# A linear-attention block gated by a mixer: the tables of order and places replaced by tables searched over replays with late adding transfers

## The chip, the cores and the metric

The kernel runs on one core of a Trainium2 chip. The metric is the device time of one execution in microseconds (us). The engines are PE (TensorE, matrix products), ACT (ScalarE), DVE (VectorE), POOL (GpSimd) and SP (SyncE, which here only issues transfers). Each engine takes its own instructions strictly in the order in which the kernel issues them; engines wait for one another by semaphores. A transfer (DMA) is issued by an engine and lands some microseconds later. An *adding transfer* is one that POOL issues and that adds what it brings to what the destination tile holds already; the program calls it a gather.

## The reference

The input x has 2048 rows of 512. It is normalised, sent through linear attention with 32 heads and, beside that, through a mixer with a token shift; the one gates the other.

```python
xn = _layernorm(x)
# s: linear attention, 32 heads of width 16
pq, pk = phi(q), phi(k)            # phi(t) = t+1 if t>0 else exp(t), plus 1e-6
kv = einsum("bhsd,bhse->bhde", pk, v);  z = einsum("bhsd->bhd", pk)
s = (einsum(pq, kv) / (einsum(pq, z) + 1e-6)) @ wo
# g: mixer
h  = gelu(_layernorm(xn) @ w1)     # four quarters of its columns, shifted by +1, -1, +2, -2 rows
x1 = xn + shifted(h) @ w2
g  = silu(x1 + gelu(_layernorm(x1) @ w3) @ w4)     # w3: 512 x 1376
return x + s * g
```

## The kernel before, in words

**How the work is cut.** The 2048 rows are four blocks of 512, each four tiles of 128. Products are kept at full accuracy by splitting each factor into a rounded high part and a remainder (names that end in h and l): three matmuls for each product, all through the helper `mm` (L133). Where it can, the kernel computes a two-by-two block product with seven products in place of eight (`pair_kq` for keys and queries, `seven` for the mixer and the up projection, `down_late` for the down projection).

**The operations.** The program doesn't issue instructions as it goes. It fills a `Plan`: each helper records an operation with its engine, and the plan works out which tiles it reads and writes. The helpers, with the lines that the profile shows: `mm` L133 (PE), `act` L155 (ACT), `tt` L178, `ts` L183 and `stt` L188 (DVE, or POOL where said so), `load` L194, `store` L199 and L201, `fetch` L206 (all three on SP) and `gather` L212 (POOL, the adding transfer). In all there are 5664 operations: 3315 on PE, 860 on DVE, 845 on ACT, 153 on POOL and 491 on SP.

**The order and the places.** At the end stand two tables written out by hand. `ORDER_OF_ALL` (from L1600) lists the numbers of all 5664 operations; `PLACES` lists, for each of the 1782 tiles, which buffer of its pool it gets (90 buffers of tag p, 6 of h, 12 of sm, 2 of w, 2 of ab, and 4 + 4 PSUM banks acc and mm; -1 where there is nothing to choose). `emit` goes through the table of order and issues each operation on its engine; so each engine's own order is the table with the other engines left out. A tile that takes over a buffer has to wait for the readers of the tile that had it before.

**Two stretches that the prediction speaks of.**

Around 80 to 105 us the kernel handles the key and query products of block 3 (rows 1536 on) and gets ready for the mixer on block 0. The tile xt3_c holds a quarter of block 3 transposed (`load_u`): SP loads it, POOL adds the row of means (`nrow`) by a gather (operations 744, 748, 752 and 756 for c = 0 to 3), and ACT and DVE split it into u3_ch and u3_cl (operation 745 is ACT's u3_0h). `forms_x` makes the sums xs3_n from them (operation 788 is ACT's xs3_0h). `pair_kq(12)` multiplies them: operation 899 is PE's first product with u3_0h, 906 the one with xs3_0h. `load_halo` fetches two small pieces of `nrow` into hm (operations 1134 and 1135 on SP), POOL adds them to hal (1136), and ACT rounds hal to halh (1137). `scale_x` computes the mean terms nm1 on POOL (762 and 763) that ACT needs for the normalisation of x12 (764). Operation 610 is an adding transfer of one key tile into zacc, 1122 the one into xt0_1, a tile of block 0 that `load_u(0, 1)` loads a second time.

Around 440 to 460 us the down projection of block 3 (`down_late`) is on. Its results xo14 and xo15 get the stored x1 added by gathers (operations 4938 and 4962), then `gate` takes the silu on ACT (th14, operation 4939) and multiplies by the attention on DVE (4940). Beside it `down_forms(0)` makes the factors for the next block: operation 5007 is ACT's rounding d_s40h, 5008 DVE's remainder d_s40l.

At about 199 us PE waits for ACT's o7 (operation 1798), with operation 1872 the first product behind the wait; both are in `mix2`.

Of the kernel before, what the change touches and what calls it, by code (L numbers as in the profile page):

```python
# [245 lines left out]
def linear_attn_gated_by_mixer(  # L246
# [1341 lines left out]
    for b in LINE:  # L1588
# [11 lines left out]
        0, 16, 1, 5, 20, 11, 3, 15, 12, 4, 13, 17, 2, 23, 14, 32, 6, 18, 19, 45, 44, 35, 21, 97, 22, 26, 46, 98,  # L1600
        174, 47, 53, 123, 24, 29, 48, 33, 108, 175, 25, 99, 49, 100, 34, 38, 102, 96, 124, 103, 51, 105, 41, 50,
        106, 109, 36, 107, 56, 125, 110, 27, 246, 52, 178, 126, 176, 37, 28, 101, 54, 62, 104, 301, 111, 112, 59,
        179, 30, 113, 55, 158, 10, 31, 117, 127, 118, 186, 177, 119, 142, 65, 39, 240, 159, 128, 180, 143, 114, 66,
        505, 42, 160, 40, 203, 57, 181, 161, 237, 144, 145, 43, 129, 115, 67, 474, 247, 116, 162, 130, 146, 68, 187,
        147, 260, 58, 120, 121, 248, 69, 131, 163, 182, 122, 243, 204, 70, 164, 132, 8, 165, 74, 135, 205, 264, 71,
        206, 75, 183, 63, 220, 221, 9, 188, 166, 60, 207, 7, 222, 76, 167, 223, 64, 224, 256, 225, 72, 77, 194, 61,
        148, 241, 149, 78, 189, 136, 268, 133, 137, 83, 226, 480, 238, 197, 227, 190, 84, 198, 73, 138, 150, 184,
        200, 242, 199, 79, 477, 195, 284, 85, 168, 244, 483, 228, 201, 139, 239, 86, 285, 245, 191, 169, 286, 192,
        250, 88, 287, 208, 151, 91, 89, 209, 249, 210, 196, 92, 152, 193, 134, 202, 140, 211, 80, 212, 288, 251,
        232, 81, 281, 309, 282, 170, 278, 279, 153, 185, 252, 229, 272, 303, 253, 475, 273, 255, 275, 87, 304, 280,  # L1610
        493, 171, 337, 213, 95, 302, 476, 338, 254, 276, 277, 154, 349, 214, 230, 90, 289, 481, 257, 290, 274, 305,
        155, 291, 261, 283, 172, 292, 215, 328, 269, 339, 296, 156, 325, 293, 294, 482, 306, 265, 326, 327, 310,
        321, 231, 141, 340, 319, 216, 341, 733, 342, 402, 334, 93, 233, 329, 295, 478, 404, 331, 322, 332, 313, 335,
        330, 94, 336, 217, 343, 307, 344, 317, 345, 346, 297, 403, 258, 333, 347, 484, 348, 314, 357, 354, 234, 259,
        409, 360, 355, 262, 487, 350, 405, 410, 315, 358, 361, 366, 263, 362, 406, 311, 411, 407, 412, 390, 367,
        546, 497, 413, 266, 392, 363, 82, 414, 386, 501, 547, 312, 548, 394, 408, 356, 388, 415, 416, 395, 368, 417,
        396, 364, 423, 479, 369, 397, 418, 365, 419, 485, 267, 157, 430, 431, 420, 316, 270, 421, 432, 370, 389,
        433, 359, 393, 424, 486, 422, 271, 434, 373, 425, 426, 400, 387, 427, 488, 435, 371, 428, 401, 442, 429,
        443, 318, 444, 298, 445, 391, 173, 446, 447, 308, 489, 549, 490, 550, 235, 398, 551, 492, 553, 320, 436,
        554, 727, 555, 556, 236, 399, 323, 509, 557, 1133, 558, 437, 448, 449, 450, 510, 559, 451, 438, 452, 453,  # L1620
        378, 454, 372, 579, 580, 439, 581, 455, 381, 511, 582, 552, 583, 324, 611, 494, 456, 617, 459, 440, 460,
        379, 560, 498, 461, 351, 462, 463, 382, 512, 464, 352, 561, 562, 465, 502, 299, 584, 563, 567, 469, 568,
        513, 569, 374, 620, 470, 570, 506, 571, 457, 572, 526, 377, 614, 441, 564, 300, 380, 565, 471, 724, 618,
        619, 522, 751, 621, 472, 622, 458, 612, 573, 531, 629, 385, 615, 218, 495, 616, 730, 586, 585, 491, 566,
        587, 613, 623, 496, 574, 626, 635, 466, 630, 575, 631, 588, 514, 636, 535, 589, 590, 576, 627, 591, 375,
        624, 628, 592, 499, 625, 637, 473, 542, 632, 500, 633, 593, 638, 639, 530, 640, 503, 534, 634, 532, 596,
        641, 706, 536, 709, 538, 467, 597, 598, 603, 599, 533, 600, 468, 539, 540, 649, 747, 650, 601, 518, 541,
        703, 656, 657, 725, 577, 521, 700, 642, 743, 602, 658, 537, 659, 525, 594, 660, 726, 661, 353, 643, 543,
        644, 595, 662, 645, 604, 646, 578, 507, 701, 647, 504, 675, 383, 605, 676, 677, 376, 606, 710, 678, 544,
        704, 755, 607, 679, 648, 680, 796, 545, 651, 728, 707, 508, 652, 731, 705, 668, 681, 2027, 669, 734, 702,  # L1630
        797, 384, 711, 732, 653, 885, 737, 670, 654, 529, 735, 798, 517, 671, 672, 729, 799, 685, 686, 655, 736,
        687, 688, 519, 673, 803, 738, 674, 689, 663, 690, 708, 608, 664, 800, 804, 805, 609, 806, 692, 739, 715,
        759, 740, 801, 693, 691, 718, 742, 719, 760, 712, 219, 802, 807, 808, 694, 515, 713, 1121, 714, 817, 809,
        741, 721, 761, 722, 665, 810, 762, 1134, 811, 682, 812, 666, 988, 813, 861, 748, 695, 716, 717, 818, 696,
        756, 829, 723, 830, 697, 831, 763, 720, 523, 814, 832, 744, 1135, 864, 815, 819, 752, 816, 820, 821, 870,
        776, 683, 822, 610, 833, 865, 823, 516, 867, 684, 868, 834, 824, 886, 698, 871, 862, 772, 872, 869, 520,
        836, 764, 775, 837, 524, 866, 1117, 838, 879, 887, 767, 757, 839, 825, 876, 1136, 877, 882, 785, 863, 835,
        840, 841, 749, 873, 842, 880, 1137, 881, 1138, 883, 784, 874, 853, 1122, 846, 758, 878, 745, 847, 848, 780,
        884, 667, 875, 782, 788, 849, 850, 783, 826, 899, 789, 900, 1151, 906, 843, 786, 907, 1118, 908, 746, 768,
        851, 909, 750, 910, 790, 771, 911, 901, 787, 1171, 902, 912, 827, 973, 1129, 903, 1149, 904, 794, 779, 888,  # L1640
        964, 791, 974, 905, 965, 932, 795, 753, 970, 967, 852, 699, 854, 933, 920, 913, 1147, 889, 934, 527, 921,
        781, 922, 844, 923, 792, 924, 925, 890, 1157, 935, 754, 936, 895, 971, 968, 528, 926, 1002, 897, 1003, 793,
        845, 937, 1004, 855, 939, 896, 891, 914, 915, 940, 1123, 898, 975, 966, 856, 828, 972, 941, 769, 1069, 942,
        857, 943, 1130, 1068, 1005, 969, 858, 916, 944, 917, 1125, 859, 918, 985, 1006, 945, 979, 919, 1007, 1067,
        980, 938, 976, 956, 977, 949, 989, 1150, 1124, 982, 1162, 1153, 986, 1154, 987, 1119, 957, 1009, 860, 983,
        1008, 950, 892, 951, 958, 777, 952, 984, 1103, 1010, 978, 1023, 765, 953, 1011, 1148, 1139, 766, 954, 927,
        1012, 1013, 1014, 928, 1016, 1024, 778, 1025, 929, 1017, 1126, 1018, 1015, 981, 2132, 930, 1079, 1266, 1085,
        1161, 1141, 770, 1019, 955, 1070, 1035, 1086, 1120, 1036, 959, 893, 1037, 1026, 946, 1027, 960, 2026, 1028,
        931, 773, 1087, 1104, 947, 1088, 961, 1089, 1090, 1268, 1038, 1029, 962, 1020, 1100, 894, 1155, 1039, 1159,
        990, 1160, 1040, 774, 1042, 1075, 1082, 1083, 991, 1043, 1071, 992, 1021, 1044, 993, 1131, 1045, 1041, 1046,  # L1650
        1142, 1047, 1169, 994, 1101, 1048, 1080, 1158, 1081, 1073, 1172, 1269, 1076, 1084, 1022, 1052, 1053, 1074,
        1054, 1059, 1094, 1055, 1072, 1030, 1056, 1214, 995, 1165, 1091, 1140, 1077, 1095, 1057, 1031, 963, 1200,
        1049, 1215, 1060, 1097, 1127, 1098, 1201, 1078, 1058, 1173, 1061, 1174, 1256, 1202, 1132, 998, 1175, 1267,
        1096, 1167, 1105, 1176, 1152, 1261, 1032, 1092, 1128, 1102, 1000, 1143, 1203, 1163, 999, 1186, 1146, 1062,
        1216, 1187, 1106, 1166, 1177, 1001, 1145, 1170, 1107, 1217, 2036, 1204, 1108, 1218, 1144, 1033, 1188, 1109,
        1099, 1205, 2038, 2037, 1189, 1111, 1274, 1190, 1191, 1050, 1113, 1219, 1034, 1178, 1110, 1206, 2142, 1115,
        1207, 1294, 1063, 1278, 997, 1220, 1093, 2029, 1192, 1064, 1208, 2039, 1221, 1275, 1193, 1179, 1180, 1065,
        1181, 1209, 1210, 2028, 1051, 1211, 2030, 1182, 1183, 1114, 1408, 1222, 1223, 948, 1184, 1224, 1225, 1288,
# [352 lines left out]
```

## Time and profile before

| | us |
|---|---|
| median of three executions | 501.97 (501.96, 501.97, 503.74) |
| the profiled execution | 504.37 |
| its span (first to last instruction) | 502.7 |

| engine | busy, us | share of the span |
|---|---|---|
| PE | 492.8 | 98% |
| DVE | 436.8 | 87% |
| ACT | 381.0 | 76% |
| POOL | 109.7 | 22% |

Rows of the profile read like this. In a timeline: the start in us, the duration in us, the engine, the line, the instruction, the tiles as out<-in (buffer numbers left out: xo stands for xo0 to xo15), the shape, and in square brackets how long the engine sat idle before and what it waited for. In a list of waits: who waited, for whom, the total in us, how often, and the longest. "DMA to landing" is the time from a transfer's issue to its landing. In a windows row: the stretch, its length, the busy time of PE, of weight loads, DVE, ACT and POOL (with the count of instructions), the granted PE clock, the DMA share and GB/s. Matmuls overlap, so what a PE row costs is the distance from one start to the next, and not its duration.

### The profile page before, as it was taken

To read this page: it belongs to the slowest core of one execution; us is meant where nothing else is said; L and a number is where in the kernel's file an instruction comes from. 1 tells how busy PE (TensorE), PEld (TensorE's weight loads), DVE (VectorE), ACT (ScalarE), POOL (GpSimd) and SP (SyncE) were. 2 spreads that over 40 slices of the span, in tenths; PEclk is the share of its full clock that TensorE was granted. 3 is DMA by queue.
4 is the path that set the end of the run, shared out by engine and by line. 5 is a ranking of instruction groups with operands and counts; after the bars stand their busy time and mean duration, and the time that the engine had idled before them with its cause. 6 is when DMAs were issued, how large, how long until landed. Compare 5 with 4: busy or idle time off the path is not lost.

```text
span 502.7 us, 10103 instructions
## 1 busy us (share of the span) xinstructions
PE 492.8 (98%) x3340; PEld 447.9 (89%) x3340; DVE 436.8 (87%) x860; ACT 381.0 (76%) x904; POOL 109.7 (22%) x157
## 2 busy tenths in 40 slices
PE   8999999999999999999999999999999999999996
PEld 5777777778787988988999999999999999999996
DVE  6999985688999988999999899999989979876754
ACT  5999999587976898998899777566679557556421
POOL 1674514322110222211011000000000044334330
PEclk9999999999999999999999999999999999999999
DMA  7978897999988989869798788757779989999998
GB/s 227 356 177 182 177 281 257 229 238 254 303 224 259 209 277 217 220 172 267 213 250 260 276 254 255 223 176 213 242 240 303 322 175 259 272 204 265 274 236 237
DMA packets 90925, 121.59 MB, mean 242 GB/s; under 512 B 10745, under 2 KB 42393, under 8 KB 90873
## 3 DMA queue, kind: packets, MB, share of 16 engines
q1 hardware_dynamic: 78488, 98.93, 60.9%
q0 software_dynamic: 12384, 22.03, 26.7%
q8 instruction: 26, 0.43, 0.3%
q14 instruction: 27, 0.21, 0.1%
HBM read 74.63 MB, written 42.09 MB: 232 GB/s over the span
## 4 chain that ended last, share of the span: by engine, by line
PE 51%; DVE 10%; DMA 5%; issue 3%; ACT 3%; POOL 1%; SPq 0%; DVEq 0%; ACTq 0%; POOLq 0%
PE pb L133 10%; PE pbd L133 9%; PE pe L133 5%; PE ped L133 5%; PE pbs L133 4%; PE h L133 3%; PE pad L133 3%; PE pa L133 3%; PE pbm L133 2%; DMA xo<-x1d 2%; PE pes L133 2%; PE a L133 2%; DMA y_0t<-y_0d 2%; PE pem L133 1%; PE pas L133 1%
## 5 line engine op out<-in xcount | busy, mean ns | idle before, releaser
L212 POOL DMA_DIRECT2D xo<-x1d x12 | 11.7, 989 | 151.4 <-DVE xo L178 133.4
L155 ACT ACTIVATE th<-xo 128x512 f32<-128x512 f32 (+1 forms) x16 | 9.8, 615 | 29.1 <-DMA xo<-x1d 13.5
L212 POOL DMA_DIRECT2D o<-xnd x16 | 14.1, 896 | 73.6 <-DVE o L178 42.1
L212 POOL DMA_DIRECT2D zacc<-ke x12 | 11.7, 975 | 47.5 <-DMA zacc<-ke 7.9
L212 POOL DMA_DIRECT2D th<-in_x x14 | 12.8, 940 | 32.1 <-DVE th L188 12.8
L212 POOL DMA_DIRECT2D xt<-nrow x16 | 15.2, 1169 | 7.3 <-DMA nrow<-ar 3.4
L155 ACT ACTIVATE ht<-ht 128x512 f32<-128x512 f32 x16 | 9.7, 624 | 4.8 <-DVE ht L178 4.7
L155 ACT ACTIVATE y<-o,nm,rs 128x512 f32<-128x512 f32 x16 | 12.7, 810 | 0.0
L183 POOL TENSOR_SCALAR w<-mv 128x4 f32<-128x4 f32 (+2 forms) x10 | 2.9, 292 | 42.5 <-ACT sq L155 42.2
L188 DVE SCALAR_TENSOR_TENSOR th<-th,so 128x512 f32<-128x512 f32 x8 | 5.5, 689 | 7.6 <-ACT th L155 7.6
L178 DVE TENSOR_TENSOR ht<-h,abc 128x512 f32<-128x512 f32 x16 | 10.9, 685 | 1.2 <-PE h L133 1.0
L155 ACT ACTIVATE sq<-o,mv 128x512 f32<-128x512 f32 x16 | 11.6, 723 | 0.2
L188 DVE SCALAR_TENSOR_TENSOR qz<-pq,zb 128x512 f32<-128x512 f32 x16 | 10.9, 682 | 0.6 <-ACT zb L155 0.4
L155 ACT ACTIVATE pa<-pb 128x256 f32<-128x256 f32 x20 | 7.4, 371 | 5.0 <-PE pb L133 4.7
L188 DVE SCALAR_TENSOR_TENSOR pq<-pq,rd 128x512 f32<-128x512 f32 x16 | 10.9, 682 | 0.2
L1283 DVE TENSOR_REDUCE den<-qz 128x32 f32<-128x512 f32 x16 | 10.8, 676 | 0.2
L155 ACT ACTIVATE p<-pe 128x256 f32<-128x256 f32 x20 | 7.5, 377 | 4.5 <-PE pe L133 4.5
L452 POOL TENSOR_TENSOR rs<-w,nhalf 128x4 f32<-128x4 f32 (+2 forms) x10 | 10.3, 1031 | 0.8
L155 ACT ACTIVATE sq<-o 128x512 f32<-128x512 f32 x16 | 10.0, 626 | 0.1
L155 ACT ACTIVATE x<-x,nm,rs 128x512 f32<-128x512 f32 x12 | 9.4, 803 | 0.0
L155 ACT ACTIVATE u<-pb 128x256 f32<-128x256 f32 x20 | 7.6, 380 | 2.3 <-PE pb L133 2.3
L188 DVE SCALAR_TENSOR_TENSOR qr<-qe,qi 128x512 f32<-128x512 f32 x10 | 6.8, 688 | 2.8 <-PE pbx L133 2.7
(2020 smaller groups left out, 2477.8 us busy)
## 6 DMA issues: line engine op xcount, KB each, us to landing
w_s<-in_w SPq DMA_DIRECT2D x23, 256.0 KB, 4.6
x<-in_x SPq DMA_DIRECT2D x16, 256.0 KB, 5.3
xt<-in_xt SPq DMA_DIRECT2D x16, 256.0 KB, 4.5
xnd<-x SPq DMA_DIRECT2D x16, 256.0 KB, 3.6
xt<-nrow POOLq DMA_DIRECT2D x16, 256.0 KB, 7.5
pqd<-qr SPq DMA_DIRECT2D x16, 256.0 KB, 4.4
pq<-pqd SPq DMA_DIRECT2D x16, 256.0 KB, 3.2
o<-xnd POOLq DMA_DIRECT2D x16, 256.0 KB, 5.3
```

What stands on the lines that cost most here:

```text
L133: lambda: nc.tensor.matmul(out.get(), lhs.get(), rhs.get(), start=start, stop=stop, skip_group_check=more))
L155: nc.scalar.activation(out.get(), src.get(), func, scale=get(scale), **kw)
L178: self.vec(eng, out, [a, b], lambda: self.e(eng).tensor_tensor(out.get(), a.get(), b.get(), op=op), True)
L183: lambda: self.e(eng).tensor_scalar(out.get(), a.get(), get(s1), get(s2), **kw), False,
L188: lambda: self.nc.vector.scalar_tensor_tensor(out.get(), a.get(), get(s), b.get(), op0=op0, op1=op1),
L212: lambda: self.nc.gpsimd.dma_start(out.get(), get(src), accum_op=ALU.add), mb=mb)
L452: lambda: g.tensor_tensor(out.get(), src.get(), nh.get(), op=ALU.pow))
L1283: pl.add("DVE", .6, .68, [t], [den], lambda: nc.vector.tensor_reduce(den.get(), t.get().rearrange("p (h d) -> p h d", d=DH), axis=AX.X, op ...
```

## The change

Both tables are replaced, and nothing else: the functions that record the operations are the same to the letter. The few words that came with the change: the same operations, with tables of order and places searched on over replays in which some adding transfers land several microseconds late.

Taken engine by engine, 2783 of PE's 3315 operations stand at another position (by 3.6 positions on average, 33 at most), 591 of DVE's 860 (1.5 and 17), 607 of ACT's 845 (1.9 and 30), 357 of SP's 491 (2.2 and 17) and 42 of POOL's 153 (0.5 and 6). Of the 1782 places 1469 differ. The core of the diff, with the lines that hold the operations named above (the last pair is the first change in `PLACES`):

```diff
@@ -1597,376 +1597,376 @@
...
-        741, 721, 761, 722, 665, 810, 762, 1134, 811, 682, 812, 666, 988, 813, 861, 748, 695, 716, 717, 818, 696,
-        756, 829, 723, 830, 697, 831, 763, 720, 523, 814, 832, 744, 1135, 864, 815, 819, 752, 816, 820, 821, 870,
-        840, 841, 749, 873, 842, 880, 1137, 881, 1138, 883, 784, 874, 853, 1122, 846, 758, 878, 745, 847, 848, 780,
-        884, 667, 875, 782, 788, 849, 850, 783, 826, 899, 789, 900, 1151, 906, 843, 786, 907, 1118, 908, 746, 768,
...
+        696, 810, 811, 515, 1134, 817, 752, 720, 741, 665, 812, 813, 744, 519, 722, 666, 829, 717, 697, 756, 723,
+        864, 682, 520, 861, 870, 748, 818, 830, 683, 819, 610, 814, 516, 820, 1135, 821, 822, 1117, 1122, 867, 823,
+        868, 831, 684, 832, 762, 815, 836, 763, 816, 865, 837, 838, 523, 862, 833, 824, 834, 524, 863, 871, 764,
+        775, 853, 877, 878, 886, 780, 846, 745, 988, 847, 667, 784, 848, 1129, 875, 785, 757, 880, 881, 788, 758,
+        899, 900, 749, 884, 789, 906, 826, 907, 1171, 782, 849, 779, 786, 908, 1136, 850, 787, 790, 851, 1118, 964,
+        746, 909, 768, 910, 750, 911, 970, 912, 901, 783, 902, 827, 903, 794, 904, 973, 791, 967, 1137, 905, 965,
...
-        1798, 1831, 1710, 1669, 1832, 1803, 1870, 1848, 1749, 1833, 1871, 1872, 1850, 2008, 1873, 1874, 1835, 1886,
...
+        1831, 1737, 1798, 1868, 1869, 1870, 1669, 1832, 1803, 2008, 1848, 1833, 1871, 1872, 1710, 1850, 1873, 1874,
...
-        5062, 4938, 5012, 5084, 4998, 5085, 5086, 5353, 5113, 5063, 5064, 5058, 5065, 5329, 5087, 5001, 4988, 5099,
-        5149, 4963, 5122, 5123, 5161, 5005, 5131, 5162, 5132, 4964, 5163, 5007, 5164, 5165, 5133, 5134, 5011, 5166,
-        4965, 5167, 5135, 4939, 5136, 5168, 5093, 5124, 5137, 5138, 5150, 4940, 5125, 5151, 5380, 5169, 5170, 5126,
-        5111, 5008, 5033, 5139, 4941, 5171, 5172, 5127, 5152, 5387, 5173, 5174, 5175, 5368, 5153, 5140, 5176, 5141,
...
+        5062, 5053, 4938, 4998, 5099, 5079, 4984, 5080, 5129, 5081, 5031, 5082, 5083, 4879, 5054, 5084, 5085, 5100,
+        4939, 5166, 5167, 5355, 5149, 5168, 5007, 5137, 5150, 5151, 5347, 5124, 5380, 5169, 4996, 5170, 5171, 5172,
+        4880, 5093, 5138, 5139, 5140, 5141, 5142, 5125, 5173, 5126, 5008, 5174, 5175, 5152, 5153, 5143, 4940, 5127,
...
-        -1, 79, 76, -1, 1, 3, 2, 14, 0, 35, 50, 53, 58, 60, 55, 62, 76, 81, 71, 74, 84, 88, 59, 65, 77, 83, 19, 20,
...
+        -1, 79, 21, -1, 1, 3, 2, 14, 0, 35, 50, 53, 58, 60, 55, 62, 76, 81, 71, 74, 84, 88, 59, 65, 77, 83, 19, 20,
...
```

711 rows, old and new, of tables (ORDER_OF_ALL, PLACES) are left out of this document.

## The prediction

> **What bounds the kernel now.** I read the page's first part, then the list of TensorE's waits, then the timelines of every engine around the longest waits.
>
> ```profile
> span 502.7 us, 10103 instructions
> PE 492.8 (98%) x3340; PEld 447.9 (89%) x3340; DVE 436.8 (87%) x860; ACT 381.0 (76%) x904; POOL 109.7 (22%) x157
> ```
> ```profile
> PE pbx L133 <- ACT u_0h L155: 1.1, 1, 1.1
> PE warm L133 <- POOL ones L368: 1.0, 1, 1.0
> PE k L133 <- ACT u_1h L155: 0.8, 1, 0.8
> ```
> ```profile
> 498.08 0.28 PE L133 MATMUL pbd<-w_l1h,dl1l 96*128 96x256 f32 x1
> ```
>
> PE is busy 492.8 of 502.7 us, so 9.9 us is idle in all. The waits list splits it: 1.0 (for the constant) and 0.8 (the first u_1h) lie at the very start, and after the last matmul (498.08 + 0.28 = 498.36) the tail takes 502.7 - 498.36 = 4.3. What is left between start and tail is 9.9 - 1.0 - 0.8 - 4.3 = 3.8 us. The tables of order hold the same 3315 PE operations in both kernels, the head (first seven PE operations) and the last fifty PE operations stand as they stood, so start and tail are taken as unchanged and only the 3.8 us are at stake. Each wait costs a little more than its idle time, because the matmuls before it drain; the first of the two places below lists 1.10 and loses 1.26, so 0.16 more. With four such waits of weight (three at the places below and the one that stays) the whole that an order could win is about 3.8 + 4 x 0.16 = 4.4 us. Against the median of 501.97 that is a floor of 497.6.
>
> **Place one, 99 us.** Matmuls of width 512 start 0.23 apart where nothing waits (98.86 to 99.09).
>
> ```profile
> 98.86 0.39 PE L133 MATMUL pbx<-kq_t41h,u_3h 128*128 128x512 f32 x1
> 99.09 0.40 PE L133 MATMUL pbx<-kq_t41l,u_3h 128*128 128x512 f32 x1
> 100.58 0.50 PE L133 MATMUL pbx<-wk_0h,u_0h 128*128 128x512 f32 x1 [1.10 <-ACT u_0h L155]
> ```
> ```profile
> 99.23 0.26 ACT L155 ACTIVATE halh<-hal 128x64 fp32r<-128x64 f32 x1 [2.59 <-POOL hal L178]
> 99.40 0.61 ACT L155 ACTIVATE qe<-qk 128x512 f32<-128x512 f32 x1
> 99.92 0.61 ACT L155 ACTIVATE u_0h<-xt 128x512 fp32r<-128x512 f32 x1
> ```
> ```profile
> 84.73 0.20 POOL L178 TENSOR_TENSOR nm<-mv,ns 128x4 f32<-128x4 f32 x1
> 85.72 1.85 POOL L212 DMA_DIRECT2D xt<-nrow  x2 [0.79 <-PE pex L133]
> 87.65 0.22 POOL L183 TENSOR_SCALAR nm<-nm 128x4 f32<-128x4 f32 x1
> 87.93 1.80 POOL L212 DMA_DIRECT2D xt<-nrow  x2
> 98.72 0.49 POOL L178 TENSOR_TENSOR hal<-hal,hm 128x64 f32<-128x64 f32 x1 [8.09 <-issue]
> 100.03 0.88 POOL L212 DMA_DIRECT2D xt<-nrow  x1
> ```
> ```profile
> DMA to landing us min/median/max: 5.7/8.4/11.1
> ```
> ```profile
> DMA to landing us min/median/max: 4.2/7.2/8.5
> ```
>
> The start of the matmul of u_0h comes 100.58 - 99.09 = 1.49 after the one before it: 1.49 - 0.23 = 1.26 us lost. It waits for ACT's rounding u_0h. ACT works in order, and its rounding of the halo, halh, stood ahead of u_0h: halh sat 2.59 idle for POOL's sum hal, which sat 8.09 for the two small loads of hm (first of the two landing rows: 5.7 and 11.1 us). The second landing row is that of the eight transfers into xt between 84 and 104 us, loads and gathers.
>
> **Place two, 457 us.** Matmuls of width 256 start 0.12 apart.
>
> ```profile
> 445.17 1.22 POOL L212 DMA_DIRECT2D xo<-x1d  x1
> 446.24 1.93 POOL L212 DMA_DIRECT2D xo<-x1d  x1
> ```
> ```profile
> DMA to landing us min/median/max: 6.1/7.7/9.3
> ```
> ```profile
> xo<-x1d POOLq DMA_DIRECT2D x12, 256.0 KB, 6.3
> ```
> ```profile
> 451.86 0.62 ACT L155 ACTIVATE d_s40h<-d0f_s40f 128x512 fp32r<-128x512 f32 x1
> 455.61 0.63 ACT L155 ACTIVATE th<-xo 128x512 f32<-128x512 f32 x1 [3.13 <-DMA xo<-x1d]
> 456.14 0.36 ACT L155 ACTIVATE u2d<-pbd 128x256 f32<-128x256 f32 x1
> ```
> ```profile
> 456.27 0.69 DVE L188 SCALAR_TENSOR_TENSOR th<-th,so 128x512 f32<-128x512 f32 x1 [2.66 <-ACT th L155]
> 456.88 0.68 DVE L178 TENSOR_TENSOR d_s40l<-d0f_s40f,d_s40h 128x512 fp32r<-128x512 f32 x1
> ```
> ```profile
> 456.19 0.28 PE L133 MATMUL pbd<-wu_40l,d_s1xh 128*128 128x256 f32 x1
> 456.56 0.38 PE L133 MATMUL pbd<-wu_01h,d_s30h 128*128 128x256 f32 x1
> 457.13 0.28 PE L133 MATMUL ped<-wf_b220l,d_s40h 128*128 128x256 f32 x1
> 457.62 0.39 PE L133 MATMUL ped<-wf_b220h,d_s40l 128*128 128x256 f32 x1 [0.21 <-DVE d_s40l L178]
> ```
>
> The adding transfer into xo14 (POOL, 446.24) landed 9.3 us later, at 455.5; the other one in this stretch took 6.1, and the median of all twelve is 6.3. ACT's th14 waited 3.13 for it, DVE's th14 behind that 2.66. Behind ACT's th14 stood u2d, and PE lost 456.56 - 456.19 - 0.12 = 0.25; behind DVE's th14 stood d_s40l, and PE lost 457.62 - 457.13 - 0.12 = 0.37. Together 0.62.
>
> **The change part by part.** Nothing is added or removed: the same 5664 operations, with the same instruction each, so the busy time of PE (492.8) has no term. What changes is which operation stands ahead of which on each engine, and which buffer a tile has (1469 of 1782 places), that is, which earlier reader a write has to outwait.
>
> *Halo behind u_0h.* halh moves nine ACT positions later, behind u_0h and xs_0h. Those two no longer stand behind POOL's 98.72. What is late next is u_0h's own input, its adding transfer. POOL now issues block 3's four gathers in the order 2, 0, 3, 1, all ahead of the two small nm steps; the last of the four was issued by 87.93 + 1.80 = 89.7 before, and the new order takes no longer to that point (the steps of 84.73 and 87.65, 0.20 and 0.22, go behind it). With 7.2 us, the median of xt's row, all four are there at 96.9, with 8.5 at 98.2; ACT needs about 0.6 for each. xt3_1, which was among the earlier ones, is now last; its products come after those of u_0h and xs_0h on PE, 0.23 each after 99.3, and with the median landing u3_1h is done at 97.5. On 8.5 it would be done at 98.8, still ahead. So the 1.26 goes in full. halh itself is needed only by the halo's copies for a later stage, and the rows show no waiter of it beside POOL's second half. Bounds: 0 (u_0h is as late for another reason) to 1.26; I take 1.26, as no row shows u_0h's input late at its old place: ACT's wait was for hal, not for xt.
>
> *xo14's gather one or more places earlier.* On POOL, xo15 and xo14 now go out so that xo14's takes at latest the place of the row at 445.17, 1.07 earlier. With the same 9.3 it lands at 454.4; ACT's th14 is done at 455.1, and d_s40h, which now stands behind th14 (it was at 451.86, ahead), at 455.7. DVE's d_s40l now stands ahead of th14's multiply and is done at 455.7 + 0.7 = 456.4, 0.7 before 457.13, the start of the last matmul ahead of the one that needs d_s40l. So both losses go, 0.62, if the transfer behaves as in this execution. It need not: an execution where xo14's landing takes the 6.3 of the median has it at 452.5, before anything waits for long, and loses nothing here. One late landing in a profiled execution 2.40 us over the median is thin evidence for the median; I count the half, 0.31. The cover is thinner than before in one respect: d_s40h now has th14 ahead of it, so from a landing of about 10 us at the new place PE waits for d_s40h as well.
>
> *The rest.* I expect the many other moves (on average 3.6 positions on PE, 1.5 on DVE) to be neutral, between -2.5 (all that remains of the 4.4 after these two places) and +2.5 (two new waits of the size of place one).
>
> *What stays.* One more stall is left alone by the tables.
>
> ```profile
> 198.84 0.40 PE L133 MATMUL m<-wo_0h,kvrl 128*128 128x512 f32 x1
> 199.97 0.39 PE L133 MATMUL pam<-w_b21h,ha122h 128*128 128x256 f32 x1 [0.73 <-ACT o L155]
> ```
> ```profile
> 200.00:225.00 25.00, 24.69 (x169) 22.33 (x170) 22.58 (x44) 23.76 (x67) 6.08 (x9) 1.00 0.81 208
> 450.00:475.00 25.00, 24.70 (x206) 24.29 (x206) 17.50 (x36) 13.06 (x30) 7.79 (x9) 1.00 1.06 264
> ```
>
> PE loses 199.97 - 198.84 - 0.23 = 0.90 there, and the order of ACT and PE around it is the same in both tables. Behind it DVE is busy 22.58 and ACT 23.76 of 25 us, so this stretch has little room to take up a head start.
>
> **Sum.** -1.26 - 0.31 = -1.57, from the median: 501.97 - 1.57 = 500.4. The profiled execution itself took 504.37 (span 502.7 and 1.67 around it), which is 2.40 above the median; with both places in full it would be 504.37 - 1.88 = 502.5.
>
> **Against the Trainium skill.** The landing rows are 6.1, 6.3 and 9.3 us for 256 KB. The Trainium skill, page "DMA: Bandwidth & Descriptors", section "Anatomy of one DMA — SWDGE (gpsimd) path", fits a transfer that GpSimd issues as about 2.0 us and its bytes over 436e3; for 262,144 bytes that is 2.6 us, an estimate by that page. By it nothing would land late in either order, the change would have nothing to gain, and the time would stay at 501.97. The trace disagrees at every row of this form that is shown here, by more than a factor of two.
>
> **The rivals.**
>
> *No gain (0.18).* In a median execution the landings are shorter than in the profiled one: 5.7 instead of 11.1 for the second load of hm, 5.4 less, would have hal start at 98.7 - 5.4 = 93.3, halh with it, and u_0h not held. Then place one isn't lost in the median either, and taking it away gives nothing. Or the head start at 99 us is used up where DVE and ACT are nearly full. For it: the profiled execution is 2.40 over the median. Against: ACT and POOL wait 2.59 and 8.09, and 2.6 us would have to vanish. Time: 501.97 less at most place two's half, 501.7 to 502.0. The fit of the Trainium skill's page leads to the same time.
>
> *More (0.20).* The order was rearranged almost everywhere, and the other small waits go too. All but the stall at 199 us: 4.4 - 0.9 = 3.5, so 501.97 - 3.5 = 498.5.
>
> *A gather that blocks POOL (0.12), slower.* POOL now has the gather into xt0_1 (row 100.03) ahead of the nm steps (rows 84.73 and 87.65). POOL works in order, and that gather must wait for the plain load of the same tile:
>
> ```profile
> 85.21 0.41 SPq L194 DMA_DIRECT2D xt<-in_xt  x1
> ```
> ```profile
> L155 ACT ACTIVATE x<-x,nm,rs 128x512 f32<-128x512 f32 x12 | 9.4, 803 | 0.0
> ```
>
> Behind nm stand on ACT three normalisations (0.80 each), two exponentials (0.61 each) and then u_0h (0.61). If the load lands L after 85.21, u_0h is done at 85.21 + L + 0.88 + 0.42 + 2.4 + 1.2 + 0.61 = 90.7 + L. PE needs it at about 99.3, so this decides from L = 8.6, which is just over the longest of the xt row, 8.5. Hm's 11.1 gives 11.1 - 8.6 = 2.5 lost in place of 1.26: 501.97 - 0.31 - 1.26 + 2.5 = 502.9. Three us more (as xo14's 9.3 stands over 6.3), 14.1, gives 505.9, which is this rival's price. Against it: the median of xt's landings is 7.2. The row of 100.03 shows only that the load took under 14.8.
>
> **How the numbers follow.** Forecast 0.50 at 500.4, more 0.20 at 498.5, no gain 0.18 at 501.8, the blocked POOL 0.12 at 505.9 (502.9 at its near end). The low end is the floor, 497.6. The high end is 503.7, which the blocked POOL reaches at L = 11.9; above it I leave 0.10, and some below the floor and in the rest. A difference from no change can be told from about 0.5% on, 2.5 us: below 499.46 lie most of "more" and about a fifth of the forecast's spread, 0.18 + 0.10 = 0.28; above 504.48 nearly all of the blocked POOL, 0.11; between them 0.61.
>
> **What would show it.** Right: the matmul of u_0h follows its forerunner by about 0.23 (not 1.49), with halh later on ACT; th14's landing leaves no wait in front of d_s40l; and the 0.90 at the pam matmul stands as before. Wrong: idle time before x12 on ACT or before nm on POOL near 90 us for an xt0_1 load; a new wait of PE over 1 us for any ACT rounding; PE idle between start and tail still near 3.8.

## The result, and the profile after

The new kernel takes 498.3 us in the median of five executions (497.6 to 499.99), the kernel before, run beside it, 503.41 (501.96 to 503.74): a ratio of 0.991, with a 95% interval of 0.9884 to 0.9937. Measured a second time on the chip of the last experiments (`e12_new_again` below) it was 497.95 against 502.63, a ratio of 0.9917 (0.9899 to 0.9935). So the change takes 0.8 to 0.9% off, 4.2 to 4.5 us at the level of 502. (The ratio isn't that of the two medians: in the first measurement these stand 5.1 apart, in the second 4.7.) The profiled execution of the new kernel took 497.6, the lowest of its five; that of the kernel before, 504.37, was longer than any of the five beside it. So the two profiles lie further apart, 6.8 us, than the kernels do.

First the head of the page and TensorE's list of waits (who, for whom, us in total, times, longest):

```profile
span 495.9 us, 10093 instructions
PE 488.3 (98%) x3340; PEld 447.6 (90%) x3340; DVE 436.8 (88%) x860; ACT 380.7 (77%) x904; POOL 108.8 (22%) x157
```
```profile
PE k L133 <- ACT u_1h L155: 1.2, 1, 1.2
PE warm L133 <- POOL ones L368: 1.0, 1, 1.0
PE m L133 <- DVE o L178: 0.4, 1, 0.4
PE pam L133 <- ACT o L155: 0.4, 1, 0.4
```

Only four entries are left: the two of the start, and two of the stall near 196 us that both kernels have. The span is 6.8 us shorter, and 4.5 us of that is *busy* time of PE (492.8 to 488.3), although the matmuls are the same. So "busy" holds waiting too (a row of width 512 lasts 0.39 where the next starts after 0.23), and the idle column doesn't show the whole loss.

Place one in the new kernel, in the timelines of PE and ACT: u_0h's matmul follows its forerunner by 0.23 (it was 1.49), and ACT starts on u_0h 1.5 us before that matmul, at 96.52, and has it 0.9 ahead.

```profile
97.77 0.39 PE L133 MATMUL g<-k10h,x10l 128*128 128x512 f32 x1
98.00 0.39 PE L133 MATMUL pbx<-wk_0h,u_0h 128*128 128x512 f32 x1
```
```profile
96.52 0.62 ACT L155 ACTIVATE u_0h<-xt 128x512 fp32r<-128x512 f32 x1
```

The transfers did not become punctual. The landing row of the tiles xt, 80 to 106 us, says 6.0, 7.7 and 10.0 us (before: 4.2, 7.2 and 8.5):

```profile
DMA to landing us min/median/max: 6.0/7.7/10.0
```

Place two is gone as well. xo15 and xo14 go out at 435.59 and 438.45 (before: 445.17 and 446.24), land 6.0 and 6.7 later, at 441.6 and 445.1, and ACT gets to them 3.5 and 1.3 us after that, with no idle time in front (POOL, the landing row of xo, ACT):

```profile
435.59 0.86 POOL L212 DMA_DIRECT2D xo<-x1d  x1 [3.90 <-ACT xo L155]
438.45 0.86 POOL L212 DMA_DIRECT2D xo<-x1d  x1
```
```profile
DMA to landing us min/median/max: 6.0/6.4/6.7
```
```profile
445.12 0.62 ACT L155 ACTIVATE th<-xo 128x512 f32<-128x512 f32 x1
446.47 0.62 ACT L155 ACTIVATE th<-xo 128x512 f32<-128x512 f32 x1
```

The same shows in the group of these sixteen ACT operations. Its row (busy and mean, then idle time before it and who ended it), first before, then after: 13.5 us of waiting for the adding transfers into xo, and then none of it among the releasers listed. Other profiles told below agree: 8.7 and 8.0 us in two with the old order there, 0.8 in the second one of the new kernel.

```profile
L155 ACT ACTIVATE th<-xo 128x512 f32<-128x512 f32 (+1 forms) x16 | 9.8, 615 | 29.1 <-DMA xo<-x1d 13.5 <-DVE xo L188 8.2 <-DVE xo L178 6.0
```
```profile
L155 ACT ACTIVATE th<-xo 128x512 f32<-128x512 f32 (+1 forms) x16 | 9.8, 614 | 14.0 <-DVE xo L188 7.8 <-PE pbd L133 3.1 <-DVE xo L178 2.2
```

**Where the time went.** For every matmul I took the distance to the next start and subtracted what that form takes where nothing waits (about 0.233 for width 512 and 0.118 for 256). What is left is PE's loss, waits hidden in "busy" included. The level of a row hangs on these values, as a thousandth of a us on each of 2549 matmuls of width 256 is 2.5 us; the differences between columns hang on them by two or three tenths at most. In stretches of 20 or more us of PE's work (not of the clock, so that the kernels can be laid side by side), in us; a star marks stretches in which the kernel of that column has the old order:

| PE's work, us | before | e1 | e6 | e5 | after | after, again |
|---|---|---|---|---|---|---|
| 0–20 (start) | 2.26* | 2.81* | 2.54* | 2.23 | 2.35 | 4.16 |
| 20–40 | 0.73* | 0.79* | 0.78* | 0.21 | 0.45 | 0.15 |
| 80–100 (place one) | 1.78* | 0.38 | 1.30* | 0.23 | 0.13 | 0.26 |
| 140–160 | 1.02* | 1.02* | 0.15 | 0.94* | 0.22 | 0.22 |
| 160–200 (the stall) | 3.28* | 3.19* | 3.55 | 1.77* | 3.11 | 3.06 |
| 200–240 | 1.63* | 1.62* | 0.50 | 1.63* | 0.38 | 0.40 |
| 240–420 | 3.12* | 2.10* | 2.62 | 2.39* | 2.79 | 2.84 |
| 420–440 (place two) | 1.64* | 0.35* | 0.23 | 0.28* | 0.25 | 0.71 |

The kernels e1, e5 and e6 are told below. Each column is one execution: 504.37, 501.67, 499.93, 497.85, 497.6 and 499.8 us. In all, from the first matmul to the last, the profiled kernel before loses 17.4 us and the new one 10.9; the stretches left out of the table hold 1.9 and 1.2 of that.

### The profile page after: what moved, and what is told of

Same layout as the page of the kernel before. It is cut to its first block, busy times and chain, and to the rows that moved or that the text cites. A ratio compares the mean times of both kernels' runs of the same rounds, so it can differ in the third digit from the quotient of the medians.

```text
span 495.9 us, 10093 instructions
## 1 busy us (share of the span) xinstructions
PE 488.3 (98%) x3340; PEld 447.6 (90%) x3340; DVE 436.8 (88%) x860; ACT 380.7 (77%) x904; POOL 108.8 (22%) x157
## 4 chain that ended last, share of the span: by engine, by line
PE 95%; DMA 2%; DVE 1%; ACT 1%; SPq 0%; issue 0%; ACTq 0%; DVEq 0%
PE pbd L133 12%; PE pb L133 12%; PE g L133 9%; PE h L133 9%; PE pbx L133 7%; PE ped L133 6%; PE pe L133 6%; PE pbs L133 5%; PE pbm L133 4%; PE pad L133 3%; PE pex L133 3%; PE pa L133 3%; PE pes L133 2%; PE a L133 2%; PE q L133 2%; PE k L133 2%
## 5 line engine op out<-in xcount | busy, mean ns | idle before, releaser
L212 POOL DMA_DIRECT2D xo<-x1d x12 | 10.5, 875 | 152.0 <-DMA d0f_s10f<-hd 128.3
L212 POOL DMA_DIRECT2D xt<-nrow x16 | 15.5, 1287 | 13.5 <-DMA xt<-in_xt 6.1
L1283 DVE TENSOR_REDUCE den<-qz 128x32 f32<-128x512 f32 x16 | 10.9, 682 | 0.2
L188 DVE SCALAR_TENSOR_TENSOR qz<-pq,zb 128x512 f32<-128x512 f32 x16 | 10.9, 682 | 0.1
L155 ACT ACTIVATE xo<-pbd 128x256 f32<-128x256 f32 x6 | 2.3, 385 | 8.6 <-PE pbd L133 8.6
L155 ACT ACTIVATE sq<-x,mv 128x512 f32<-128x512 f32 x12 | 8.5, 711 | 0.0
```

The costliest lines, as they stand in the source:

```text
L155: nc.scalar.activation(out.get(), src.get(), func, scale=get(scale), **kw)
L188: lambda: self.nc.vector.scalar_tensor_tensor(out.get(), a.get(), get(s), b.get(), op0=op0, op1=op1),
L212: lambda: self.nc.gpsimd.dma_start(out.get(), get(src), accum_op=ALU.add), mb=mb)
L1283: pl.add("DVE", .6, .68, [t], [den], lambda: nc.vector.tensor_reduce(den.get(), t.get().rearrange("p (h d) -> p h d", d=DH), axis=AX.X, op ...
```

## The experiments

Every ratio is to the kernel before, run beside it on the same chip; a median's difference is to its median there (502.42, 501.9 and 502.63 us for the three groups).

**e1_halo_later: one part of the change alone.** The kernel before with halh and POOL's second half of it behind xs_0h:

```diff
-        840, 841, 749, 873, 842, 880, 1137, 881, 1138, 883, 784, 874, 853, 1122, 846, 758, 878, 745, 847, 848, 780,
-        884, 667, 875, 782, 788, 849, 850, 783, 826, 899, 789, 900, 1151, 906, 843, 786, 907, 1118, 908, 746, 768,
+        840, 841, 749, 873, 842, 880, 881, 883, 784, 874, 853, 1122, 846, 758, 878, 745, 847, 848, 780,
+        884, 667, 875, 782, 788, 1137, 1138, 849, 850, 783, 826, 899, 789, 900, 1151, 906, 843, 786, 907, 1118, 908,
```

> The kernel before with one edit: ACT's rounding of the halo, halh, and POOL's second half of it stand behind ACT's u_0h and xs_0h; all places as before. Theory A (the order of ACT's queue made the 1.26 us wait at 99 us): the wait of u_0h goes, with the 0.16 behind it, so 1.3 to 1.4 us less than before and nothing else moves. Rival (u_0h's input or a later stretch is as late): within 0.4 us of before, and TensorE waits elsewhere near 100 us.

Measured: 502.02 us (12 executions), ratio 0.9991 (0.9973 to 1.0009): 0.5 us less, between 1.4 less and 0.5 more. In the profile the wait is gone, and a part of it comes back 30 us later, where a matmul of the mixer on block 0 now waits for an ACT operation (before: 0.05 idle there, 0.22 lost; here 0.31 idle, 0.47 lost):

```profile
99.91 0.40 PE L133 MATMUL pbx<-wk_0h,u_0h 128*128 128x512 f32 x1
129.76 0.50 PE L133 MATMUL h<-u_0h,w_0h 128*128 128x512 f32 x1 [0.31 <-ACT zi L155]
```

So the mechanism of place one is as told, and 1.4 of the 1.78 us in that row of the table goes; what it is worth in the median isn't settled by this run, as its interval holds the expected value and zero.

**e2_new_front, e3_new_back, e4_places: the tables cut in two, and the places alone.** The first two join the order of one table to the rest of the other, with the cut near 118 us; tiles whose buffer was taken got the one that had been free longest, counted in the table's order (672 and 760 tiles). The third leaves the order of before and deals all places in that way. In form (e3 is the mirror image, with 1007):

```diff
-    ORDER_OF_ALL = BEFORE
+    ORDER_OF_ALL = NEW[:1024] + [n for n in BEFORE if n not in NEW[:1024]]
```

> The new order up to about 118 us (its first 1024 operations, with their places), then the order of before. Theory A (each wait is a local matter of the order, and what is won at one place is kept): the spacing of TensorE's matmuls lost 2.0 us more in the kernel before up to there than in the new one, so 2.0 us less than before. Rival (a head start is used up by the waits that follow): under 0.7 us less. Theory B (the new places, not the order, made the gain): about as many places are new as not, so any size, not tied to the stretch.

> The counterpart: the order of before up to about 118 us (its first 1007 operations, with their places), then the new order. Theory A: the rest of the 6.5 us by which the two profiled executions differ in spacing, 4.4 us less than before, with the 1.26 at 99 us still there. Rival (place one is the whole gain): under 1 us less.

> The order of before, untouched, with 1508 of the 1782 places dealt anew (each tile gets the buffer that has been free longest). Theory A: the order makes the time, so within 0.7 us of before, with the waits at 99, 199, 281 and 457 us in their places. Theory B (places make the waits, by the readers that a new tile has to outwait): a change of over 1.5 us, and the waits at 281 us or 99 us gone or others in their stead.

Measured: 536.71 us, 1.0699 (1.0672 to 1.0725); 536.41 us, 1.0679 (1.0657 to 1.0702); 527.64 us, 1.0504 (1.0483 to 1.0526). My expectation failed outright: places dealt without care cost 25 us under an unchanged order. The profile of e4_places, in VectorE's waits for transfers, shows what kind of wait that is:

```profile
DVE d_s40l L178 <- DMA out<-th: 5.8, 1, 5.8
DVE u_2l L178 <- DMA zacc<-ke: 4.0, 1, 4.0
```

d_s40l reads neither out nor th: it was given the buffer of a tile th whose store to the output was still under way, and u_2l that of a tile ke that an adding transfer was still reading. A tile that a transfer reads is free when the transfer has landed, not when it was issued, and "free longest in the table's order" doesn't know that. So e2 and e3 say nothing on where the gain lies. They were made again.

**e5_new_front2, e6_new_back2: the cut with the places kept.** Same cut, but behind it the places of the second table under one renaming of the buffers, so that tiles alive at the cut keep theirs and every takeover of a buffer behind the cut is one that the second table had, but for some two dozen. In the order, in form (e6 is the mirror image, with 1182):

```diff
-    ORDER_OF_ALL = BEFORE
+    ORDER_OF_ALL = NEW[:1196] + [n for n in BEFORE if n not in NEW[:1196]]
```

> The new order and places up to about 135 us (the first 1196 operations), then the order of before with the places of before under other buffer numbers: one renaming of the buffers for the whole rest, so that the tiles alive at the cut keep theirs and no buffer is taken over sooner after its last reader than it was. Theory A (the order of the in-order queues; each loss is local, the places are only what the order needs): up to there the profiled kernel before lost 2.2 us more than the new one, so 1.5 to 2.5 us less than before. Theory B (giving back: late transfers cost the same somewhere else): within 0.7 us of before. Theory C (the places make the time): as in the first front, tens of us more.

> The counterpart: before up to about 138 us (1182 operations), then the new order with its places under renamed buffers. Theory A: the rest of the gain, 2.5 to 4 us less than before, with the 1.26 at 99 us still there; together with the front it makes the whole 4.5 to 5. Theory B: front and back together stay under 2.5. Theory C: tens of us more.

Measured: front 499.35 us, 0.9956 (0.9935 to 0.9976), 2.2 us by the ratio (1.2 to 3.3); back 500.09 us, 0.9964 (0.9944 to 0.9983), 1.8 us (0.9 to 2.8). Together 4.0, of the 4.2 to 4.5 of the whole. Within these intervals the gain adds up by stretches, as theory A has it; the back's share came out under the 2.5 that was expected. The table above shows what repeats. In the stretches 20–40, 140–160 and 200–240 every profile with the old order there loses nearly the same (0.73 to 0.79, 0.94 to 1.02, 1.62 and 1.63), every one with the new order a third of it or less, but for 0.45 in one. One such wait, in the timelines of before, e1 and e6, where the order there is the old one:

```profile
33.94 0.50 PE L133 MATMUL g<-k2h,x2h 128*128 128x512 f32 x1 [0.29 <-ACT k2h L155]
```
```profile
34.55 0.50 PE L133 MATMUL g<-k2h,x2h 128*128 128x512 f32 x1 [0.29 <-ACT k2h L155]
```
```profile
34.05 0.50 PE L133 MATMUL g<-k2h,x2h 128*128 128x512 f32 x1 [0.29 <-ACT k2h L155]
```

The same 0.29 each time: that is order, not chance. Place two is the opposite: with the old order 1.64 in one profile, 0.35 and 0.28 in two others. It is lost where that landing is late enough: xo14's took 9.3 us in the first, 8.8 and 7.8 in the other two. With the new order it took 6.7 and 5.8, so the order has a part in the landing itself.

**e7_pool_old: the adding transfers' order put back.** The new kernel with POOL's 153 operations in their old order, 42 of them at another position; everything else new.

```diff
-    POOL: xt3_2, xt3_0, xt3_3, xt3_1, zacc, xt0_1, nm1, nm1
+    POOL: nm1, xt3_1, xt3_3, nm1, xt3_0, xt3_2, zacc
...
-    POOL: xo15, th12, xo14, th13, d0f_s4xf, d1f_s4xf, th15, th14
+    POOL: th12, th13, xo15, d0f_s4xf, xo14, th15, th14, d1f_s4xf
```

> The new kernel with one engine put back: POOL's 153 operations, the adding transfers among them, in the order of before; the other four engines and all places new. Theory A (what counts is what stands behind a late transfer on ScalarE and VectorE, not when POOL issues it): within 1 us of the new kernel, so 3.5 to 5 us less than before, with a wait of at most 0.6 near 445 us, where the transfer for xo14 goes out behind that for th13 again. Rival (the earlier issue of the adding transfers is the gain): 2 us or more is lost against the new kernel, at 99 us and near 445 us.

Measured: 510.53 us, 1.0166 (1.0139 to 1.0193), 8.6 more than before and, by the ratios, about 13 more than the new kernel. Theory A as I had put it falls. About two thirds of the loss is in the down projection (POOL, then ACT, then PE):

```profile
453.64 0.86 POOL L212 DMA_DIRECT2D th<-in_x  x1 [6.05 <-issue]
458.64 0.86 POOL L212 DMA_DIRECT2D th<-in_x  x1 [4.13 <-DVE d_s4xl L178]
459.17 1.22 POOL L212 DMA_DIRECT2D d1f_s4xf<-hd  x1
```
```profile
466.45 0.42 ACT L155 ACTIVATE d_s4xh<-d1f_s4xf 128x256 fp32r<-128x256 f32 x1 [6.94 <-DMA d1f_s4xf<-hd]
```
```profile
468.01 0.39 PE L133 MATMUL pad<-wf_b210h,d_a120h 128*128 128x256 f32 x1 [2.35 <-ACT d_a120h L155]
```

The transfer for d1f_s4xf stands behind those for th15 and th14 again, which go out only at 453.64 and 458.64 (the second after a wait for VectorE), and goes out itself at 459.17. Some 2 us of the loss there come after these waits: PE then ran at half its clock for 6.8 us (last section). The other four engines are ordered for an early landing (in the new kernel's trace it goes out at 441.9). The old order of POOL was no worse in its own company: before has no such wait. So POOL's order is a part of the change that the others need; this run doesn't say what it gains alone.

**e8_o7_first, e9_y_later: the stall that stays.** In both kernels ACT's o7 stands behind two roundings, yb210h and yb110h, that wait for a transfer into y_0t; a second such transfer, into y_1t, follows. I moved what PE needs ahead of them, first o7 and p1 (and yt1f behind o8 on VectorE), then also the copies mq and u2, p5, and hs32l and hs42l. By the names, the ACT order of the new kernel and of e9:

```diff
-    yb210h, yb110h, o7, sq24, p1m8, mq11, mq00, mq01, yb220h, yt10h, w4_2h, u2m8, p5m8, yb120h
+    o7, sq24, p1m8, mq11, mq00, mq01, yb210h, yb110h, w4_2h, u2m8, p5m8, yb220h, yt10h, yb120h
```

> The new kernel with one more edit at the stall that both kernels have at about 196 us: ScalarE's o7 and p1 of the next product ahead of the two roundings yb210 and yb110 that wait for a transfer, and VectorE's sum yt1f behind o8. If that stall too is a transfer in front of an in-order queue: TensorE's 0.58, 0.31 and 0.60 there go, 1.2 to 1.5 us less than the new kernel, 5.5 to 6.5 less than before. Rival (given back behind it, where ScalarE and VectorE are nearly full, until about 228 us): within 0.5 us of the new kernel.

> The new kernel with the stall at 196 us taken on more fully: on ScalarE o7, p1 and the three copies mq ahead of yb210 and yb110, and u2 and p5 of that product ahead of yb220 and yt10; on VectorE o8, hs32l and hs42l ahead of yt1f; so that nothing that TensorE needs stands behind the two transfers y_0t and y_1t. If the stall is only a matter of the queue: 1.2 to 1.7 us less than the new kernel run beside it. Rival (given back by 228 us, where ScalarE and VectorE are nearly full, as when only o7 went first): within 0.5 us of the new kernel, with the loss again between 196 and 230 us.

Measured: e8 499.05 us, 0.9942 (0.9921 to 0.9963); e9 498.36 us, 0.9924 (0.9907 to 0.9941), beside it the new kernel 497.95, 0.9917. No gain: the rival. The wait moves on, in e8 to u2, which stands behind ACT's yb220h, and that waits for y_1t; in e9 to the next copies mq, which stand behind yt10h, and that waits for VectorE's yt1f, which I had put behind hs42l (rows of TensorE's waits, e8 and e9):

```profile
PE pbm L133 <- ACT u2m L155: 1.4, 1, 1.4
```
```profile
PE pbm L133 <- ACT mq L155: 1.3, 1, 1.3
```

The stall isn't in every execution, and the table shows it: 1.77 in the row 160–200 of e5, which has the old order there, against 3.1 to 3.6 in the others. In e5's trace the transfer was there in time, ACT takes yb210h without idle time, and PE's pam matmul waits for nothing (ACT in before and in e5):

```profile
198.50 0.63 ACT L155 ACTIVATE yb210h<-y_0t 128x512 fp32r<-128x512 f32 x1 [1.60 <-DMA y_0t<-y_0d]
```
```profile
193.96 0.63 ACT L155 ACTIVATE yb210h<-y_0t 128x512 fp32r<-128x512 f32 x1
```

So this loss hangs on a landing too. e8 and e9 moved what stands behind the transfer, and not the transfer; an earlier issue of it wasn't tried.

**e10_late_before, e11_late_after: later adding transfers on purpose.** Both kernels with 28 copies of 256 KB that nobody waits for, issued by POOL ahead of the adding transfers into xt and xo:

```diff
+            if n in self.late:
+                self.extra(n)
             op.emit()
...
+        d = pools["dram"].tile([P, 512], F32, tag=f"late{n}", name=f"late{n}")
+        nc.gpsimd.dma_start(d[:, :], x[:P, :])
```

> The kernel before with 28 transfers more that nobody waits for: POOL issues a copy of 256 KB of the input into scratch memory ahead of each of the 28 adding transfers into the tiles xt and xo, so that each of these goes out about 1 us later and lands later still. Theory A (the new order stands late adding transfers better): 3 to 8 us over before. Rival (both stand them alike, the gain came from other waits): the same surcharge as the new kernel's within 1 us.

> The new kernel with the same 28 transfers more at the same 28 adding transfers. Theory A: at least 2 us less surcharge than the kernel before has by them, 0 to 3 us over the new kernel. Rival: the same surcharge within 1 us.

Measured: 517.42 us, 1.029 (1.0265 to 1.0315), 14.8 over before; 514.57 us, 1.0238 (1.0213 to 1.0263), 16.6 over the new kernel. Theory A falls here as well, and both surcharges are far over what was expected: the new order stands this kind of lateness no better (the 1.8 us between the surcharges are within what the intervals leave open). It keeps a lead of 2.9 us. The load was also heavier than meant: where four gathers follow one another each is put off by one more copy, and both kernels then wait for the sums of the tiles xt (TensorE's waits, e10 and e11):

```profile
PE pbx L133 <- ACT u_0h L155: 3.4, 1, 3.4
PE pex L133 <- ACT xs_0h L155: 2.6, 1, 2.6
```
```profile
PE pex L133 <- ACT xs_0h L155: 5.5, 3, 2.7
PE pbd L133 <- ACT p1d L155: 2.1, 1, 2.1
```

**e12_new_again: the new kernel once more.**

> The new kernel once more, unchanged, beside the three others on the same chip. The first measurement's ratio of 0.991 should come again within 0.003; every theory expects it. It tells how far one profile of the same kernel lies from another: if losses of a few tenths come and go with the landing times, the listed waits differ from those of the first profile except for the start and the stall at 196 us.

Measured: 497.95 us, 0.9917 (0.9899 to 0.9935). Of the waits only the start and the stall are as in the first profile; small ones come and go (0.71 in place two, 0.25 the first time), and the start lost 4.16 in place of 2.35. There PE waited 1.84 for u_1h, not 1.24, and then had half its clock for 3.4 us: nine matmuls started in a time in which the first profile has fifteen (first profile, then this one; the first of the last three figures is the granted clock).

```profile
7.90:11.30 3.40, 3.40 (x15) 2.52 (x14) 3.40 (x8) 2.58 (x5) 0.00 (x0) 1.00 1.03 321
```
```profile
7.90:11.30 3.40, 3.40 (x9) 2.60 (x9) 3.40 (x8) 2.10 (x5) 0.00 (x0) 0.50 0.99 294
```

## Why the prediction was right or wrong

The measured median lies in the range, and the direction was right. The size was not: 1.57 us forecast, 4.2 to 4.5 measured. What came is the rival "more": all listed waits but those of the start and the stall are gone. That its 498.5 lies so near the 498.3 is in part luck: it took 3.5 us of idle time off a median of 501.97, while PE's idle time fell by 2.3 (9.9 to 7.6) between the two profiles, its busy time by 4.5, and the median of the kernel before was 502.6 to 503.4 beside the new one.

- **The bound.** PE does set the time, the tail is unchanged (4.3 both times; forty, not fifty, of PE's last operations stand as they stood), and the stall stays. But the floor was worked out from PE's idle column, 3.8 us and a little for each wait. That was too tight: the spacing of the matmuls shows 17.4 us lost before (2.3 of it at the start), and 4.5 of the 6.8 us between the two spans left PE's busy time. The floor of 497.6 was not broken by the median, but it wasn't one: single executions came under it (497.35 the lowest).
- **Halo behind u_0h, 1.26.** The mechanism was right, and so was "what is late next": the last of block 3's gathers came with room. The stretch lost 1.30 and 1.78 with the old order and 0.13 to 0.38 without that wait. Not foreseen: with this move alone a quarter of a us came back at the mixer's first matmul, which in the new kernel it doesn't; by what in e1 was not separated.
- **xo14's gather, 0.62 counted half.** Right in kind: it is a chance loss, seen in one of three profiles with the old order. By these three, a third would have been nearer. Its gather goes out 7.8 us sooner on the clock, but 5.1 of that is the lead that the whole kernel has by then; against PE's work it moved by 2.7, where the prediction had 1.07 at the least. The landing was shorter as well, 6.7 us, where the prediction kept the 9.3.
- **"The rest … neutral".** This is the step that failed. The stretches 20–40, 140–160 and 200–240 lose 0.5, 0.8 and 1.2 us less (means of the profiles with the one order and the other): 2.5 us of small waits that come back in every profile with the old order there. With place one's 1.3 and place two's 0.4, less the 0.2 that 240–420 loses more, that is 4.0, what the two halves measured together. But this leaves out the start and the stall, where by the same means the new order loses 0.4 and 0.5 *more*; they range from 2.2 to 4.2 and from 1.8 to 3.6 whatever the order, and with them the sum is 3.1. So which rows make the gain is shown, and about 1 us of its size stays open. The list of TensorE's waits before had shown two of the small ones, and the list of e1 has the same two lines; I had priced only the two places that were large.

```profile
PE g L133 <- ACT k2h L155: 0.3, 1, 0.3
PE pe L133 <- DVE ht L178: 0.2, 1, 0.2
```

- **No gain.** It needed place one to be absent in the median, and the losses of the other stretches to be small or given back. Stretch by stretch they stayed won: front and back add up. The fit of the Trainium skill's "DMA: Bandwidth & Descriptors" (section "Anatomy of one DMA — SWDGE (gpsimd) path"), by which nothing lands late, was beside the point: the landings are 6.0 to 10.0 us in the new kernel too.
- **The blocked POOL.** xt0_1's gather went out at 88.94 and nm at 89.50 in the trace after, so its load was there in time; the order has the risk, and it didn't come.
- **Places.** Costed at nothing, and rightly for these tables; but e4_places shows what they could have cost: an unchanged order with other places is 25 us slower.

What the change's words promise, an order that stands late transfers, is half shown. ACT's waits for the transfers into xo were 13.5, 8.7 and 8.0 us in three profiles with the old order, 0 and 0.8 in two of the new kernel; yet a general delay costs both kernels alike, and the larger part of the gain is the ordinary small waits.

## What to carry to other kernels

Where one engine sets the time, price a reordering from the start-to-start spacing of its instructions over the whole trace, and not from its few longest waits or its idle column: the small waits that repeat were worth more here than the two large ones. Compare two or three profiles of the same order before a wait is counted, because some are there each time to the hundredth (0.29) and others in one execution of three. An order and its buffers are one thing: a buffer whose last reader is a transfer is free when that transfer has landed, and one engine's order put back alone cost 13 us.

## What the runs showed of the hardware

After some long waits PE went on at half its clock. In e10 the wait of 3.36 us that ended at 109.29 was followed by matmuls of width 512 that start 0.43 apart, not 0.23, and the granted clock in that stretch is 0.50; in e11 the same after 2.66 us, for about 3 us of work.

```profile
109.29 0.79 PE L133 MATMUL pbx<-wk_0h,u_0h 128*128 128x512 f32 x1 [3.36 <-ACT u_0h L155]
109.88 0.63 PE L133 MATMUL pbx<-wk_0l,u_0h 128*128 128x512 f32 x1
110.31 0.63 PE L133 MATMUL pex<-kq_t10h,xs_0h 128*128 128x512 f32 x1
```
```profile
109.30:114.60 5.30, 5.30 (x13) 4.13 (x14) 4.11 (x8) 3.88 (x9) 3.02 (x4) 0.50 0.99 226
```
```profile
109.50:112.30 2.80, 2.80 (x7) 2.22 (x8) 2.71 (x7) 2.20 (x4) 1.73 (x4) 0.50 1.06 326
```

In e10 this cost another 2.6 us (thirteen times 0.20). In e7 the wait of 2.35 at 468.01 had such a tail too, from 469.4 on: matmuls of width 256 start 0.21 apart there, not 0.12. In e4_places a wait of 2.73 us that ended at 112.81 had none (e7, then e4_places):

```profile
469.40:476.20 6.80, 5.15 (x25) 4.91 (x24) 4.74 (x11) 1.87 (x5) 0.59 (x1) 0.50 0.59 150
```
```profile
112.00:120.00 8.00, 7.20 (x31) 5.74 (x32) 5.71 (x9) 2.64 (x5) 2.62 (x3) 1.00 0.71 163
```

Over all the profiles of this case, the first 20 us and the end left out, each of the seven waits of 3.0 us or more (3.03 to 4.25) was followed by the half clock; of the fifteen from 1.7 to 2.8 us eight were, the shortest of 1.78 (e2), and seven were not, the longest that of 2.73. So in this range the length of the wait alone doesn't decide it, and why one has the tail and another not wasn't found out. The half clock lasted 3.4 to 3.5 us or twice that each time. The Trainium skill, page "TensorE: Matmul & The Clock Gate", section "Part 1: The HAM clock gate (the "warmup" mystery)", states that the clock halves after an idle window of about 3.4 us and comes back after as long a busy one. The halving, its factor and the 3.4 us agree; but here waits from 1.78 us on were enough at times.
